# Four tiles in the first chunk, two in the second, and a fourth accumulator in the layer-1 banks

## The chip, the cores and the metric

The kernel runs on one core of a Trainium2 chip. The metric is the device time of one execution in microseconds (us), from the first to the last instruction with what lies around them. A run is repeated, and the median is taken.

## The reference

Windowed attention (half of the heads with a plain window of 32 keys, half with a window dilated by 4) feeds a token mixing of rank 32 and a two-layer network with a ReLU.

```python
scores = scale * np.matmul(q, k.transpose(0, 1, 3, 2))      # 8 batches, 8 heads, 576 tokens, 64 wide
mask_plain = (rel >= 0) & (rel < window)
mask_dil = (rel >= 0) & (rel < window * dilation) & (rel % dilation == 0)
...
x = softmax(np.where(masks, scores, -1e9)) @ v               # heads side by side: (8, 576, 512)
h = x.transpose(0, 2, 1) @ U @ V                             # U: 576x32, V: 32x576
u = x + h.transpose(0, 2, 1)
ch = np.maximum(u @ w_ch1, 0.0) @ w_ch2                      # w_ch1: 512x2048, w_ch2: 2048x512
return u + ch
```

U, V and the two weight matrices arrive as 64-bit numbers. The kernel narrows them itself, and it splits the operands of the large products into a high and a low part, so that each product is three products.

## The kernel before

The 8 x 576 tokens are 36 tiles of 128 rows. The network runs over **chunks** of 3 tiles, 12 in all; each chunk goes through 16 **steps f** of 128 hidden units. In a step, layer 1 (`layer1`, line 914) is 12 products of 128x128 weights with the chunk's 384 columns into a bank `ph`; ScalarE takes the ReLU into `hh` (L919), and VectorE the low part into `hl` (L920). Layer 2 (`layer2`, line 931) is three products of 512 columns for each tile into that tile's accumulator `acc`. The order is layer 1 of f, then layer 2 of f-1. The eight banks of the accumulation memory are three for `acc`, two for `ph` and three (`ps`) for everything else.

Chunk 0 is special in three ways. The weights are loaded and prepared in it: 32 pieces, two for a step, each fetched by a DMA into a buffer `raw` (`fetch64`, lines 189 and 191), narrowed by ScalarE (L198, L199), shifted by VectorE (L203), added by VectorE or GpSimd (`add_low`, L205) and split into high and low (L209, L211, L212). `weight_step`, called twice a step, does one stage each of four pieces in turn; `AHEAD` says how many pieces ahead a fetch is issued, and `RAWS` how many buffers `raw` there are, so that a fetch waits until the piece `RAWS` before it has been added. Second, the attention of batch 0 (`first_batch`) has been done ahead of it. Third, the attention of batch 1 runs inside it: nine groups, each with scores `s` (L405), a softmax on VectorE and ScalarE, a transpose `ptp` (L439), the products `pv` with the values `v` (L462) and `place`, which divides and puts the result into the tiles; the dilated half goes to `xp` and from there in up to six small DMAs to the tiles (L496, the scatter). Then come the low-rank products `t` (L541, from `xhl`, L511) and `m` (L565), whose result is added to the tile (L567).

All DMAs are issued by SyncE (SP), one after the other. Up to the end of chunk 0 the order on every engine is that of the code (`manual_schedule`). Where in it the work beside the network stands is set by `queue`: entries with a position, taken out by `slot()` in the gaps between groups of products. A position of 0 is the start of chunk 0 and 1 its end. Group i of batch 1 stands at `STEP0 + STEP1 * i`, the low-rank parts by `AFTER`, the way of batch 0's dilated half through memory at `leave` (L770) and `come` (L775), and batch 2 between `lo` and `hi`. From chunk 1 on a scheduler orders the work; batches 2 to 7 run inside the chunks 1 to 9.

`V1` says which columns of V come with the first of two small pieces.

Of the kernel before, what the change touches and what calls it, by code (L numbers as in the profile page):

```python
# [143 lines left out]
def attention_moe_kernel(ctx: ExitStack, tc: tile.TileContext, qk0, qk2, vv, masks, wide, ident, ut, vt, uv, w1, w2, out):  # L144
# [32 lines left out]
    def fetch64(i):  # L177
        src, n = pieces[i][0], pieces[i][1]
        if 2 * F_LAST <= i - NSMALL:
            raw = [xpool.tile([P, DM], I32, tag="x", name=f"raw{i}_{h}") for h in range(2)]  # L180
# [4 lines left out]
        for h, r in enumerate(raw):
            r = r[:, 0:step]
            if len(src.shape) == 3:
                k = src.shape[1] // len(raw)
                nc.sync.dma_start(out=r.rearrange("p (a b) -> p a b", a=k), in_=src[:, h * k:(h + 1) * k])
            else:  # L190
                nc.sync.dma_start(out=r, in_=src[:, h * step:(h + 1) * step])
# [273 lines left out]
    def place(g, pv):  # L465
# [29 lines left out]
        for t, to, n, r in sorted(moves) if b > 0 else ():  # L495
            nc.sync.dma_start(out=x_tile(t)[to:to + DIL * (n - 1) + 1:DIL, HALF_D:], in_=xp[r:r + n])  # L496
# [185 lines left out]
    def first_batch():  # L682
# [38 lines left out]
        t_first(0, 0)
        turn_dilated(2)
        t_evict(0, 1)
        tp[8] = turn_pe(8, state.pop(8)[0])
# [7 lines left out]
        turn_plain(0, 0)  # L732
        turn_plain(0, 1)
        t_first(2, 0)
        turn_plain(0, 2)
        for t in range(CT):
            turn_plain(1, t)
# [12 lines left out]
        for k in (0, 1):  # L750
            mix_turned(k)
        for k in (0, 1):
            split_u(k, 0)
        for k in (0, 1):
            split_u(k, 1)
        narrowed(w1)
        add_low(w1, nc.gpsimd)
# [293 lines left out]
```

## Time and profile before

| | |
|---|---|
| median of 3 runs | 1029.66 us (1026.68 to 1031.23) |
| the profiled execution, its own time | 1030.62 us |
| its span, first to last instruction | 1028.8 us |
| TensorE busy in the span | 988.2 us |
| VectorE, ScalarE, GpSimd busy | 586.3, 382.0, 331.8 us |
| moved by DMA | 101.36 MB |

The span is cut into 40 slices on the profile's page, with the busy share of each engine and the clock that TensorE was granted. Further views used here are the busy time by stretches (windows), the waits by engine, and the timeline, in which the matmuls of one line are merged; the time in square brackets is the idle time ahead of an instruction, and who ended it. Matmuls overlap in the records, so that the pace of a stream is the distance between starts, not the duration of one.

### The profile page before, as it was taken

The numbers are of one execution on the slowest core, as the hardware profiler recorded it, in microseconds if no ns is written. First come the engines' busy times: TensorE is split into PE (matmuls) and PEld (weight loads), VectorE is DVE, ScalarE is ACT, GpSimd is POOL, SyncE is SP. The second block draws the span as 40 slices with busy tenths as digits, with TensorE's granted clock in tenths as the row PEclk, the third lists the DMA queues.
The fourth block names the chain that finished last, engine by engine and source line by source line (L and its number), as shares of the span: only waits on it lengthen the run. The fifth ranks groups of instructions, "written<-read, shape, count | busy, mean of one in ns | idle before, by whom it ended". The sixth has DMA issues, their size and how long they took to land.

```text
span 1028.8 us, 18053 instructions
## 1 busy us (share of the span) xinstructions
PE 988.2 (96%) x5928; PEld 869.0 (84%) x5928; DVE 586.3 (57%) x1969; ACT 382.0 (37%) x937; POOL 331.8 (32%) x555
## 2 busy tenths in 40 slices
PE   7886887999999999999999999999999999999998
PEld 6576676888898888888898888988898888999997
DVE  4566686776446863766556773676646774311211
ACT  5663655444233431434323541434323441111110
POOL 4374656444032630425222540325313440000000
PEclk9988998999999999999999999999999999999999
DMA  9566543443223422333233422333223420300000
GB/s 252 171 196 206 169 145 108 117 134 89 72 73 96 138 75 75 113 97 114 64 85 97 130 82 74 106 106 112 84 74 93 126 69 21 113 1 1 31 1 31
DMA packets 95868, 101.36 MB, mean 99 GB/s; under 512 B 12480, under 2 KB 81344, under 8 KB 95776
## 3 DMA queue, kind: packets, MB, share of 16 engines
q1 hardware_dynamic: 95776, 100.21, 33.8%
q8 instruction: 48, 0.79, 0.3%
q14 instruction: 44, 0.36, 0.1%
HBM read 78.14 MB, written 17.89 MB: 93 GB/s over the span
## 4 chain that ended last, share of the span: by engine, by line
PE 83%; POOL 1%; DVE 1%; issue 1%; ACT 0%; DMA 0%; DVEq 0%; POOLq 0%; SPq 0%
PE acc L931 37%; PE ph L914 37%; PE pv L462 3%; PE s L392 3%; PE t L541 2%; PE m L565 1%; PE s L405 0%; POOL v L205 0%; POOL w1l L212 0%; DVE v L205 0%; DVE v L203 0%; POOL w2l L212 0%; PE tp L631 0%; DMA raw<-w 0%; DVE xhl L511 0%
## 5 line engine op out<-in xcount | busy, mean ns | idle before, releaser
L931 PE MATMUL acc<-w2h,hh 128*128 128x512 f32 x576 | 230.8, 401 | 0.0
L931 PE MATMUL acc<-w2l,hh 128*128 128x512 f32 x576 | 229.3, 398 | 0.0
L369 POOL TENSOR_TENSOR qks<-qkr,qks 128x160 fp32r<-128x160 f32 x192 | 103.1, 537 | 353.4 <-ACT qks L368 248.6
L920 DVE SCALAR_TENSOR_TENSOR hl<-ph,hh 128x384 fp32r<-128x384 f32 x192 | 106.2, 553 | 192.4 <-ACT hh L919 191.3
L931 PE MATMUL acc<-w2h,hl 128*128 128x512 f32 x576 | 214.2, 399 | 0.0
L919 ACT ACTIVATE hh<-ph 128x384 fp32r<-128x384 f32 x192 | 93.6, 487 | 284.4 <-PE ph L914 272.9
L914 PE MATMUL ph<-uth,w1h 128*128 128x384 f32 x768 | 171.4, 341 | 7.4 <-ACT w1h L209 6.0
L914 PE MATMUL ph<-utl,w1h 128*128 128x384 f32 x768 | 177.2, 343 | 0.0
L914 PE MATMUL ph<-uth,w1l 128*128 128x384 f32 x768 | 173.1, 341 | 1.2 <-POOL w1l L212 1.2
L428 ACT ACTIVATE p<-p,nmax 128x160 f32<-128x160 f32 (+1 forms) x288 | 109.5, 406 | 153.3 <-DVE nmax L424 152.2
L914 PEld LDWEIGHTS ph<-uth,w1h 128*128 128x128 f32 x768 | 138.2, 189 | 23.9 <-ACT w1h L209 7.3
L451 DVE STREAM_TRANSPOSE pt<-p 32x128 f32<-32x128 f32 x432 | 130.2, 301 | 18.7 <-ACT p L428 13.4
L914 PEld LDWEIGHTS ph<-uth,w1l 128*128 128x128 f32 x768 | 137.6, 190 | 2.5 <-POOL w1l L212 2.2
L914 PEld LDWEIGHTS ph<-utl,w1h 128*128 128x128 f32 x768 | 137.7, 191 | 1.7 <-issue 0.2
L931 PEld LDWEIGHTS acc<-w2h,hl 128*128 128x128 f32 x576 | 108.9, 189 | 23.2
L931 PEld LDWEIGHTS acc<-w2h,hh 128*128 128x128 f32 x576 | 109.6, 190 | 16.1
L931 PEld LDWEIGHTS acc<-w2l,hh 128*128 128x128 f32 x576 | 109.5, 190 | 15.9
L368 ACT CAST qks<-qkr 128x288 fp32r<-128x288 f32 x192 | 81.0, 429 | 95.0 <-PE s L392 56.3
L421 DVE TENSOR_TENSOR p<-s,wide_sb 128x160 f32<-128x160 f32 x192 | 60.1, 320 | 69.7 <-PE s L392 67.2
L372 POOL TENSOR_TENSOR qks<-qkr,qks 64x128 fp32r<-64x128 f32 x192 | 90.7, 472 | 15.1
L511 POOL TENSOR_TENSOR xhl<-x,xhl 128x256 fp32r<-128x256 f32 (+1 forms) x65 | 47.9, 746 | 82.3 <-ACT xhl L509 76.7
L462 PEld LDWEIGHTS pv<-v,pt 96*64 96x64 f32 x1152 | 41.4, 139 | 29.6 <-issue 11.6
(86 smaller groups left out, 901.0 us busy)
## 6 DMA issues: line engine op xcount, KB each, us to landing
qkr<-qk SPq DMA_DIRECT2D x192, 144.0 KB, 2.2
raw<-w SPq DMA_DIRECT2D x26, 512.0 KB, 4.3
v<-vv SPq DMA_DIRECT2D x126, 97.5 KB, 2.2
out<-x SPq DMA_DIRECT2D x36, 256.0 KB, 2.2
zd<-z SPq DMA_DIRECT2D x120, 64.0 KB, 2.2
xt<-zd SPq DMA_DIRECT2D x30, 256.0 KB, 2.8
k<-qk SPq DMA_DIRECT2D x18, 320.0 KB, 5.7
raw<-w SPq DMA_DIRECT2D x12, 256.0 KB, 3.8
```

Of the source, the lines that this page charges most:

```text
L368: nc.scalar.copy(out=t[:, 0:QK2], in_=raw)
L369: nc.gpsimd.tensor_tensor(out=t[:, QK2:], in0=raw[:, P:], in1=t[:, P:QK2].bitcast(F32), op=ALU.subtract)
L372: eng.tensor_tensor(out=t[lo, 0:P], in0=raw[lo, 0:P], in1=t[lo, 0:P].bitcast(F32), op=ALU.subtract)
L421: nc.vector.tensor_tensor(out=p_sb[:, u, :], in0=sp[:, 0:KW], in1=held[0][:, kind], op=ALU.add)
L428: nc.scalar.activation(out=p_sb[:, u, 0:w], in_=p_sb[:, u, 0:w], func=AF.Exp, bias=nmax[:, u:u + 1], scale=-1.0,)
L451: nc.vector.transpose(out=pt[WIN * k:WIN * (k + 1), :, rs], in_=p_sb[rs, :, o:o + WIN])
L462: nc.tensor.matmul(pv[rs, u, :], lhsT=pt[:, u, rs], rhs=loaded[g, 1, i][:, u, :], start=True, stop=True)
L511: eng.tensor_tensor(out=xl[rs], in0=x[rs], in1=xh[rs].bitcast(F32), op=ALU.subtract)
L914: nc.tensor.matmul(ph, lhsT=w[:, k, :], rhs=u[:, k, :], start=(n == 0), stop=(n == len(seq) - 1))
L919: nc.scalar.activation(out=hh, in_=ph, func=AF.Relu)
L920: nc.vector.scalar_tensor_tensor(out=hl, in0=ph, scalar=0.0, in1=hh.bitcast(F32), op0=ALU.max, op1=ALU.subtract)
L931: nc.tensor.matmul(acc[i], lhsT=h[:, ss], rhs=w, start=(f == 0 and n == 0), stop=(f == FC - 1 and n == 2))
```

## The change

The chunks are 4, 2 and then ten times 3 tiles. Chunk 0 is thus a third longer, and its layer 1 has 512 columns; chunk 1 has two tiles and 256 columns. Positions keep their unit of three tiles, so that chunk 0 ends at 4/3 and chunk 1 at 2. Chunk 0 needs a fourth accumulator, which takes one of the two banks `ph`.

```diff
-CTOK = CT * P
-NCHUNK = NTILE // CT
+CHUNKS = [range(0, 4), range(4, 6)] + [range(t, t + CT) for t in range(6, NTILE, CT)]
+CTOK = len(CHUNKS[0]) * P
+NCHUNK = len(CHUNKS)
-V1 = V0 + 3 * P
+V1 = V0 + CTOK
-AHEAD = 3
+AHEAD = 2
-AHEAD_AT = 0.9
+AHEAD_AT = (0.95, 1.3)
-RAWS = 5
+RAWS = 4
-STEP1 = 0.055
-AFTER = ((0.43, 0.015), (0.62, 0.018))
-NQ = 4
+STEP1 = 0.075
+AFTER = ((0.60, 0.022), (0.84, 0.03))
+LO2 = 1.31
+HI2 = 2.45
+NQ = 2
...
     def fetch64(i):
         if 2 * F_LAST <= i - NSMALL:
-            raw = [xpool.tile([P, DM], I32, tag="x", name=f"raw{i}_{h}") for h in range(2)]
+            raw = [work.tile([P, DM], I32, tag="qks", name=f"raw{i}_0", bufs=TB),
+                   xpool.tile([P, DM], I32, tag="x", name=f"raw{i}_1")]
...
     def place(g, pv):
-        for t, to, n, r in sorted(moves) if b > 0 else ():
+        if moves and b > 0:
+            scatter[g] = (xp, sorted(moves))
+            if b >= SPLIT:
+                spread_rows(g)
+
+    def spread_rows(g):
+        xp, moves = scatter.pop(g)
+        for t, to, n, r in moves:
             nc.sync.dma_start(out=x_tile(t)[to:to + DIL * (n - 1) + 1:DIL, HALF_D:], in_=xp[r:r + n])
...
             def pre(s=s, g=g):
-                if b < SPLIT and s + 1 < NGB:
-                    spread_q(g + 1)
+                if b < SPLIT and g - LAG - 1 in scatter:
+                    spread_rows(g - LAG - 1)
                 if s >= LAG:
                     weighted(g - LAG, held.pop(g - LAG))
             def post(s=s, g=g):
+                if b < SPLIT and s + 1 < NGB:
+                    spread_q(g + 1)
...
     def ahead(stage):
         if stage == 0:
+            held[0] = work.tile([P, len(WIDE_AT), KW], BF16, tag="mask", name="wide_sb", bufs=1)
...
-        lo, hi = 1.5 * b - 2 - LO0, 1.5 * b - 0.5
+        lo, hi = (1.5 * b - 2 - LO0, 1.5 * b - 0.5) if b > 2 else (LO2, HI2 + MARGIN)
...
-    for c in range(NCHUNK):
+    for c, tiles in enumerate(CHUNKS):
-        acc = [psum.tile([P, DM], F32, tag="acc", name=f"acc{c}_{i}", bufs=3) for i in range(CT)]
+        nt = len(tiles)
+        acc = [psum.tile([P, DM], F32, tag="acc" if i < CT else "ph", name=f"acc{c}_{i}", bufs=3 if i < CT else 2)
+               for i in range(nt)]
         def slot():
-            pos = c + slots[0] / (6 * FC - 3)
+            pos = (tiles[0] + nt * slots[0] / ((nt + 3) * FC - 3)) / CT
```

The end of `first_batch` is written in another order: the last transposes and value products come first, and the products that turn batch 0's tiles (`u`) behind them, now for four tiles.

The following rows are TensorE's at the end of batch 0, from the last scores on to where the tiles begin to be turned. `ptp8` and `pv8` are the transpose and the value products of the last of batch 0's nine groups, `t0` the low-rank product, `u2` and `u3` the turned dilated columns. Before:

```order
L462 MATMUL pv7_481<-v7_146,pt1_78 64x65 x8
L527 MATMUL t0_420<-x0_447,u32_92 32x256
L585 MATMUL u2_491<-id_sb_72,xp0_255 128x96
L585 MATMUL u2_491<-id_sb_72,xp1_292 128x96
L585 MATMUL u2_491<-id_sb_72,xp2_329 128x96
L585 MATMUL u2_491<-id_sb_72,xp3_370 128x80
L585 MATMUL u2_491<-id_sb_72,xp4_407 128x16
L439 MATMUL ptp8_500<-id_sb_72,p8_432 96x128 x4
```

and in the changed kernel:

```order
L441 MATMUL ptp8_474<-id_sb_72,p8_432 96x128 x4
L464 MATMUL pv7_484<-v7_146,pt1_78 64x65 x8
L538 MATMUL t0_420<-xp4_407,u32_92 32x256
L538 MATMUL t0_420<-x4_408,u32_92 32x256
L464 MATMUL pv8_501<-v8_148,pt0_77 64x65 x8
L596 MATMUL u2_518<-id_sb_72,xp0_255 128x128
```

`pv8` has moved ahead of all turning; before, both `u2` and `u3` stood ahead of it.

The next rows are SP's, ahead of the values `v13` of batch 1's fifth group. `raw` are weight pieces, `x<-xp` the scatter, `x<-spare` the second half of batch 0's way through memory, `k` the keys. Before:

```order
L319 DMA k15_967<-qk0 128x640
L496 DMA x4_408<-xp11_983 16x256
L496 DMA x5_780<-xp11_983 16x256 x2
L496 DMA x6_782<-xp11_983 32x256
L496 DMA x7_785<-xp11_983 16x256
L496 DMA x8_787<-xp11_983 32x256
L775 DMA x3_544<-spare_822 128x256
L775 DMA x4_408<-spare_822 64x256
L191 DMA raw18_1029<-w2 128x1024
L189 DMA raw19_1065<-w1 128x4x256
L340 DMA v13_0_1075<-vv 96x260
L340 DMA v13_1_1077<-vv 96x260
```

and in the changed kernel:

```order
L321 DMA k15_1001<-qk0 128x640
L507 DMA x4_408<-xp10_921 16x256
L507 DMA x5_900<-xp10_921 32x256
L507 DMA x6_902<-xp10_921 32x256
L507 DMA x7_905<-xp10_921 32x256
L507 DMA x8_907<-xp10_921 16x256
L191 DMA raw17_1052<-w1 128x4x256
L193 DMA raw18_1081<-w2 128x1024
L342 DMA v13_0_1092<-vv 96x260
L342 DMA v13_1_1094<-vv 96x260
```

The scatter ahead of `v13` is that of the group before, the last piece of weights ahead of it is 18 in place of 19, and the two transfers from `spare` stand further ahead.

The last rows are TensorE's where step f = 2 begins, with what the first product of layer 1 waits for in brackets; `w1h` is prepared by ScalarE. Before:

```order
L931 MATMUL acc0_2_584<-w2h_0_84,hh0_0_607 128x512
L931 MATMUL acc0_2_584<-w2l_0_85,hh0_0_607 128x512
L931 MATMUL acc0_2_584<-w2h_0_84,hl0_0_608 128x512
L914 MATMUL ph0_2_723<-uth0_69,w1h_0_82 128x384 [waits Activation_49]
L914 MATMUL ph0_2_723<-uth0_69,w1h_0_82 128x384 x3
```

and in the changed kernel:

```order
L942 MATMUL acc0_3_589<-w2h_0_84,hh0_0_631 128x512
L942 MATMUL acc0_3_589<-w2l_0_85,hh0_0_631 128x512
L942 MATMUL acc0_3_589<-w2h_0_84,hl0_0_632 128x512
L925 MATMUL ph0_2_734<-uth0_69,w1h_0_82 128x512 [waits DVE_49,Activation_49]
L925 MATMUL ph0_2_734<-uth0_69,w1h_0_82 128x512 x3
```

There are three more products of 512 columns in each layer 2, and layer 1 now waits for VectorE as well, whose `hl` of the step before has to leave the one bank `ph`.

More of the change, by code (lines that the diff above doesn't have):

```diff
@@ L77 @@
 NX = 16
-HI1 = 0.85
-W_OFF = 1000
 F_MID = 6
 F_LAST = 13
-RAWS = 5
+RAWS = 4
 VS = 4
@@ L620, in transp @@
     def transp(t):
-        c, i = divmod(t, CT)
+        c = next(c for c, ts in enumerate(CHUNKS) if t in ts)
+        i = t - CHUNKS[c][0]
         if c not in uts:
@@ L715, in first_batch @@
                 narrowed(0)
-                add_low(0, nc.gpsimd)
-                finish(0)
         w0, w1 = NSMALL, NSMALL + 1
+        tiles = CHUNKS[0]
+        tp[8] = turn_pe(8, state.pop(8)[0])
         place(6, pv.pop(6))
         pv[7] = product(7, pt.pop(7))
[L721 to L724, printed above, removed]
         copy(8)
-        finish(1)
-        t_first(1, 0)
-        turn_dilated(3)
+        for c in (1, 0):
+            t_first(ODD, c)
         place(7, pv.pop(7))
@@ L731, in first_batch @@
         narrowed(w0)
[L732 to L737, printed above, removed]
+        t_evict(0, 1)
+        finish(1)
+        turn_dilated(2)
         place(8, pv.pop(8))
         add_low(w0, nc.gpsimd)
-        send(NSMALL + 6)
+        for i in range(n - 1):
+            t_first(i, 0)
+        turn_dilated(3)
         mix_turned(2)
+        t_evict(0, 0)
         mix_turned(3)
-        t_first(3, 0)
         split_u(2, 0)
+        split_u(2, 1)
+        narrowed(w1)
+        finish(w0)
+        for k in (0, 1):
+            for t in tiles:
+                turn_plain(k, t)
+            mix_turned(k)
         split_u(3, 0)
-        split_u(2, 1)
-        t_evict(0, 0)
-        finish(w0)
+        add_low(w1, nc.gpsimd)
         split_u(3, 1)
[L750 to L757, printed above, removed]
+        for part in range(2):
+            for k in (0, 1):
+                split_u(k, part)
         narrowed(w1 + 1)
@@ L866, in attention_moe_kernel @@
     n0 = len(batch_parts(0))
-    queue = [(HI1 - MARGIN, lambda: ahead(0)), (AHEAD_AT, lambda: ahead(1))]
+    queue = [(AHEAD_AT[0], lambda: ahead(0)), (AHEAD_AT[1], lambda: ahead(1))]
     queue += [(0.15 + 0.01 * p, lambda p=p: leave(p)) for p in range(NDP)]
@@ L908, in layer1 @@
             assert NSMALL + 2 * f in finished
-            ph = psum.tile([P, CTOK], F32, tag="ph", name=f"ph{c}_{f}", bufs=2)
+            ph = psum.tile([P, CTOK], F32, tag="ph", name=f"ph{c}_{f}", bufs=2)[:, 0:nt * P]
             w1h, w1l = held_w[f][0:2]
@@ L916, in layer1 @@
                     slot()
-            hh = work.tile([P, CTOK], F32R, tag="hh", name=f"hh{c}_{f}", bufs=2)
-            hl = work.tile([P, CTOK], F32R, tag="hl", name=f"hl{c}_{f}", bufs=2)
+            hh = work.tile([P, CTOK], F32R, tag="hh", name=f"hh{c}_{f}", bufs=2)[:, 0:nt * P]
+            hl = work.tile([P, CTOK], F32R, tag="hl", name=f"hl{c}_{f}", bufs=2)[:, 0:nt * P]
             nc.scalar.activation(out=hh, in_=ph, func=AF.Relu)
@@ L927, in layer2 @@
             w2h, w2l = held_w[f][2:4]
-            for i in range(CT):
+            for i in range(nt):
                 ss = slice(i * P, (i + 1) * P)
@@ L932, in layer2 @@
                                      start=(f == 0 and n == 0), stop=(f == FC - 1 and n == 2))
-                if f < FC - 1 and i < CT - 1:
+                if f < FC - 1 and i < nt - 1:
                     slot()
-        more = list(range((c + 1) * CT, (c + 2) * CT)) if c + 1 < NCHUNK else []
+        more = list(CHUNKS[c + 1]) if c + 1 < NCHUNK else []
         for f in range(FC):
@@ L958, in attention_moe_kernel @@
             order.__exit__(None, None, None)
-        for i in range(CT):
-            t = c * CT + i
+        for i, t in enumerate(tiles):
             x = xt.pop(t)
```

13 lines of the change are left out of this document (7 added, 6 removed).

## The prediction

> **What bounds the kernel now.** I read the page first, then busy time by stretches, then TensorE's waits. The page's lines are TensorE's totals and its 40 slices of 25.7 us, with the granted clock:
>
> ```profile
> PE 988.2 (96%) x5928; PEld 869.0 (84%) x5928; DVE 586.3 (57%) x1969; ACT 382.0 (37%) x937; POOL 331.8 (32%) x555
> PE   7886887999999999999999999999999999999998
> PEclk9988998999999999999999999999999999999999
> ```
>
> From the eighth slice on TensorE is full at full clock. Only the first seven have room: the attention of batch 0 and chunk 0. The windows below cut chunk 0 in three, and the rest in two; columns are us, then busy us (and count) of PE, its weight loads, DVE, ACT and POOL, then granted clock, DMA share and GB/s.
>
> ```profile
> 43.30:102.70 59.40, 46.32 (x287) 41.04 (x288) 36.04 (x116) 30.46 (x71) 36.39 (x41) 0.85 0.64 197
> 102.70:153.90 51.20, 44.35 (x269) 36.49 (x267) 37.72 (x91) 31.11 (x72) 30.94 (x26) 0.94 0.52 158
> 153.90:181.50 27.60, 21.35 (x90) 17.63 (x91) 17.71 (x40) 13.39 (x35) 19.29 (x26) 0.88 0.38 105
> 181.50:260.00 78.50, 78.50 (x517) 68.97 (x515) 57.63 (x220) 36.18 (x90) 32.88 (x64) 1.00 0.40 111
> 260.00:1000.00 740.00, 740.00 (x4348) 657.40 (x4345) 411.43 (x1385) 245.51 (x605) 197.07 (x367) 1.00 0.28 81
> ```
>
> Chunk 0 lasts 138.2 us, of which PE is idle 138.2 - 46.32 - 44.35 - 21.35 = 26.2 us. No other engine is full there: DVE is busy 91.5 us, POOL 86.6, ACT 75.0. Behind it nothing but PE work counts. TensorE's waits in chunk 0 (us, times, longest):
>
> ```profile
> PE pv L462 <- DMA v<-vv: 8.2, 4, 3.8
> PE ph L914 <- ACT w1h L209: 6.0, 3, 2.5
> PE s L392 <- POOL qks L372: 2.9, 1, 2.9
> PE s L405 <- DVE x L567: 2.3, 1, 2.3
> PE t L541 <- POOL xhl L511: 2.0, 3, 1.2
> PE t L541 <- DVE xhl L511: 1.8, 2, 1.6
> PE ph L914 <- POOL w1l L212: 1.2, 3, 0.5
> ```
>
> **How much work chunk 0 holds.** The paces come from the chain that ended last (start, us, what), and from TensorE's timeline:
>
> ```profile
> 1013.55 2.09 PE ph L914 x12
> 1015.63 2.10 PE acc L931 x9
> ```
>
> ```profile
> 85.85 0.40 PE L565 MATMUL m<-ts,vs 128*128 128x256 f32 x2
> 86.09 0.86 PE L914 MATMUL ph<-uth,w1h 128*128 128x384 f32 x4
> ...
> 107.72 0.69 PE L462 MATMUL pv<-v,pt 96*64 96x65 f32 x16
> 108.33 1.13 PE L405 MATMUL s<-k,q 128*128 128x96 f32 x8
> 109.30 0.60 PE L439 MATMUL ptp<-id_sb,p 128*96 128x128 f32 x4
> 109.66 0.48 PE L931 MATMUL acc<-w2h,hh 128*128 128x512 f32 x1
> ```
>
> A product of 384 columns takes 2.09 / 12 = 0.174 us, one of 512 columns 2.10 / 9 = 0.233, one of 256 columns (86.09 - 85.85) / 2 = 0.12; a group of batch 1 takes 109.66 - 107.72 = 1.94. Chunk 0 before is thus 192 x 0.174 + 144 x 0.233 + 9 x 1.94 + 40 low-rank products at 0.12 + 16 others (transposes, first scores of batch 2) at about 0.12 = 33.4 + 33.6 + 17.5 + 4.8 + 1.9 = **91.2 us**. It lasts 138.2, so 47.0 us are lost: 26.2 idle, and most of the rest at half clock (1 - clock, doubled, times the windows' lengths: 17.8 + 6.1 + 6.6 = 30.5 us at half clock, up to 15 lost). An idle us costs 47.0 / 26.2 = 1.79 in all.
>
> **Term 1, the longer chunk itself.** In the changed chunk 0 layer 1 has 192 products of 512 columns, layer 2 192: 44.7 + 44.7 + 17.5 + 4.8 + 9 x 0.12 = **112.8 us**. A tile moved ahead takes 48 x 0.233 + 192 x (0.233 - 0.174) = 22.5 us away from what follows; this is no gain in work, but 22.5 us more to hide the same preparation under. Chunk 1 has 256 columns in layer 1: 192 x (0.12 - 2/3 x 0.174) = 0.8 us more.
>
> A weight load that did not fit under 256 columns would cost more. The eight scores above start every 0.97 / 8 = 0.121 us, though they stream 96 columns only, so a load of 128 columns takes about 0.12 itself and just fits. The Trainium skill's page "TensorE: Matmul & The Clock Gate", section "LDWEIGHTS (loading the stationary operand)", gives 128 / 1.2 = 107 ns, and its section "The mechanism" says that a load overlaps a running product only where the row groups differ, which full-height weights never do; by it chunk 1 would lose another 20.5 us (an estimate from the page). The trace disagrees: with fresh weights for each, 512 columns pace at 0.233 us, and 384 at 0.174, so the load is hidden.
>
> **Term 2, the start of layer 1.** The timeline before:
>
> ```profile
> 31.57 0.62 PE L527 MATMUL t<-x,u 128*32 128x256 f32 x2
> ...
> 35.98 0.69 PE L462 MATMUL pv<-v,pt 96*64 96x65 f32 x16
> ...
> 43.34 0.96 PE L914 MATMUL ph<-uth,w1h 128*128 128x384 f32 x4 [1.45 <-DVE utl L604]
> ```
>
> `pv8` stands at 35.98, 4.4 us behind the end of `pv7`'s run; in the new order two `t` (0.6 us) lie between, so it can come up to 3.8 us earlier. Behind it stand about 2.3 us more products (the turning, two tiles' plain parts), and four splits of 512 columns. Bounds: 39.5 (all of the 3.8 kept) and 45.7 (nothing of it, and 2.3 more). I take **41.0**: 35.98 - 3.8, the 7.4 us behind it without the 1.45 us in the bracket, 2.3 for the new products, and 0.6 of such waits left.
>
> **Term 3, what stays idle in chunk 0.** The largest wait is for `v`. SP's timeline at the longest, and TensorE's:
>
> ```profile
> 58.78 0.33 SPq L191 DMA_DIRECT2D raw<-w  x1
> ...
> 92.04 0.53 SPq L191 DMA_DIRECT2D raw<-w  x1
> 92.68 0.38 SPq L189 DMA_DIRECT2D raw<-w  x1
> 93.16 0.92 SPq L340 DMA_DIRECT2D v<-vv  x2
> 94.17 0.38 SPq L319 DMA_DIRECT2D k<-qk  x1
> 94.64 4.38 SPq L496 DMA_DIRECT2D x<-xp  x5
> ...
> 102.48 1.04 SPq L189 DMA_DIRECT2D raw<-w  x1
> ```
>
> ```profile
> 99.05 1.23 PE L462 MATMUL pv<-v,pt 96*64 96x65 f32 x16 [3.82 <-DMA v<-vv]
> ```
>
> From 58.78 to 103.5 SP's 33 rows sum to 37.4 of 44.7 us: issuing itself is nearly the bound there. `v13` is issued behind two pieces of weights and lands 5 us later. In the changed kernel a group comes every 0.075 in position, 6.1 gaps in place of 5.1, and a gap is 7 to a step of 5.6 us instead of 6 to one of 4.2: a group has about 7 us instead of 5.6 in full flow, for the same DMAs. Each `v` stands behind one piece of weights fewer, and the scatter ahead of it has its data. Four buffers with two pieces ahead wait for the same addition as five with three, so nothing is lost there. Of 8.2 us I keep 3 (bounds 0 and 8.2).
>
> The waits for weights (6.0 + 1.2) are at f = 1 and from f = 13 on: supply is 4.1 us of POOL for a step (two splits at 1.4, one addition at 1.3), demand falls from one step in about 6.6 to one in 8; I keep 3. Of the rest (2.9 + 2.3 + 3.8 + 2.8 at the start and the low-rank part, which is spread from 0.015 to 0.022 a piece) I keep 4.5: these are latencies, and half of them stay.
>
> New is the single `ph`: layer 1 of f+1 waits until ACT and DVE have read it. It has layer 2 of f-1 for that, 12 x 0.233 = 2.8 us. How long the reading takes shows in two places before, f = 8 and f = 13, in the last products of layer 1, ScalarE's `hh` (f = 13) and VectorE's `hl`:
>
> ```profile
> 122.71 0.86 PE L914 MATMUL ph<-utl,w1h 128*128 128x384 f32 x4
> ...
> 156.30 0.86 PE L914 MATMUL ph<-utl,w1h 128*128 128x384 f32 x4
> ```
>
> ```profile
> 160.81 0.47 ACT L919 ACTIVATE hh<-ph 128x384 fp32r<-128x384 f32 x1
> ```
>
> ```profile
> 124.13 0.56 DVE L920 SCALAR_TENSOR_TENSOR hl<-ph,hh 128x384 fp32r<-128x384 f32 x1 [3.46 <-ACT hh L919]
> ...
> 161.31 0.56 DVE L920 SCALAR_TENSOR_TENSOR hl<-ph,hh 128x384 fp32r<-128x384 f32 x1 [0.76 <-ACT hh L919]
> ```
>
> At f = 8 the lag from the end of layer 1 is 124.69 - 123.57 = 1.1 us and would be hidden; at f = 13 it is 161.87 - 157.16 = 4.7, because ACT is behind. 512 columns add some 0.3. I take 2.5 us for the 14 steps concerned (bounds 0 and 14 x (5.0 - 2.8) = 31). Together 3 + 3 + 4.5 + 2.5 = 13 us idle, x 1.79 = **23.3 us** lost. Bounds 6 and 26 us idle: 11 and 47.
>
> **Term 4, the rest.** From 181.5 to 1028.8 are 847.3 us; less 22.5, plus 0.8, plus seven products that no longer fit into chunk 0 (0.8), plus what batch 2 costs where it is denser: 1.14 positions in place of 1.3, with only 2.8 us in a step of chunk 1. DVE was at 57.63 / 78.5 = 73% there, and would be near 80%. I take 3 us (bounds 0, as PE never waits there before, and 10). That is **829.4**.
>
> Costed at nothing: NQ = 2 (a copy of the next queries has a whole group's time), the mask's buffer, 128 columns of V in the other small piece, a later GpSimd copy of the queries, which has the same 7 us.
>
> **Sum.** 41.0 + 112.8 + 23.3 + 829.4 = 1006.5 us of span; the profiled execution adds 1030.62 - 1028.8 = 1.8, and stands 1.0 above the median: **1007 us** against 1029.66.
>
> **Rivals.**
> - *All cover:* the preparation disappears under the longer chunk, 6 us stay idle, layer 1 starts at 39.5, chunk 1 loses nothing: 1007 - 12.3 - 1.5 - 3 = 990. For it: DVE's 91.5 us are no longer level with PE's work. Against: latencies stay. 0.13.
> - *Batch 2 pushes DVE over:* chunks 1 and 2 lose 10 us and the first idle more than I gave: about 1020. For it: 2.8 us a step. 0.08.
> - *Nothing covers:* the losses are chains of SP, POOL and DVE that stretch with the chunk, 47 us again: 1007 + 23.7 = 1031, no change. For it: SP's 37.4 of 44.7 us. Against: the DMAs per group don't grow. 0.11.
> - *Slower, by the one bank:* if DVE's `hl` lags as at f = 13 in all 14 steps, 31 us idle replace my 2.5, and each drags the clock down: 1007 + 28.5 x 1.79 = 1058. It decides from some 15 us of such waits, 1.1 a step, a lag of 3.9. Against: the lag of 1.1, and that ACT was behind at f = 13 because weights came late. 0.06. The Trainium skill's page "TensorE: Matmul & The Clock Gate", section "A second HAM failure mode: psum-queue depth-cycling", describes such a clock that swings as TensorE pauses briefly between groups while banks are cycled; here the clock was 1.00 in every stretch behind chunk 0, with two banks.
> - *Loads not hidden at 256 columns:* 192 x 0.121 = 23 us, back to 1030. Against: the paces above. 0.01.
>
> The forecast has 0.61, about 995 to 1019. **Range** 990 to 1024: it takes in the first two rivals, and leaves out 0.18. A difference of 0.5% (5 us) is about what a measurement can tell: faster 0.82, same 0.11, slower 0.07.
>
> **What would show it.** Layer 1 starts near 41 us; chunk 0's last product ends near 177, and the rest takes some 829 us. The waits of `pv` for `v` and of `ph` for `w1h` shrink below 3 us each; the clock in chunk 0 rises to 0.94 or more. If `ph` waits for DVE's `hl` at the head of most steps, the one bank was mispriced; if PE is idle between 180 and 290 us, chunk 1 was; if the `v` waits stand as before, SP's issuing was the bound all along.

## The result, and the profile after

The changed kernel takes 996.57 us (median of 4 runs, 994.34 to 999.47) against 1028.72 us for the kernel before on the same chip (4 runs, 1026.68 to 1031.23). The ratio is 0.969, with a 95% interval of 0.965 to 0.972: **3.1% faster**, 32 us. The profiled execution is the slowest of the four, 999.47 us with a span of 997.7.

The page of the changed kernel, TensorE's totals and slices:

```profile
PE 973.4 (98%) x5936; PEld 850.2 (85%) x5936; DVE 589.5 (59%) x1968; ACT 380.4 (38%) x936; POOL 330.7 (33%) x555
...
PE   7898999999999999999999999999999999999998
...
PEclk9999999999999999999999999999999999999999
```

Of the notches that the slices of before had in the first seven (a 6, two 7s, four 8s) one 7 and two 8s are left, and the clock stands at 9 throughout. The windows cut chunk 0 in three, and the rest in two (columns as in the prediction):

```profile
44.35:98.00 53.65, 48.01 (x284) 38.69 (x286) 36.77 (x106) 29.95 (x70) 32.63 (x39) 0.94 0.64 200
98.00:146.00 48.00, 46.03 (x289) 36.10 (x286) 40.27 (x90) 28.79 (x66) 31.29 (x28) 1.00 0.63 192
146.00:174.36 28.36, 26.56 (x121) 20.92 (x119) 21.79 (x38) 13.28 (x33) 17.88 (x21) 1.00 0.37 104
174.36:252.00 77.64, 77.17 (x560) 67.93 (x559) 57.93 (x228) 38.17 (x100) 36.33 (x69) 1.00 0.42 121
252.00:997.70 745.70, 739.29 (x4374) 657.03 (x4372) 410.75 (x1393) 245.37 (x605) 196.02 (x367) 1.00 0.29 80
```

Layer 1 starts at 44.35 us, 1.0 later than before. Chunk 0 lasts 130.0 us instead of 138.2, with a tile more in it. PE is idle in it for 5.64 + 1.97 + 1.80 = 9.4 us (26.2 before), and the clock is below 1.00 only in its first part: (1 - 0.94) x 2 x 53.65 = 6.4 us at half clock, against 30.5. (The trace also keeps the times at which the granted clock changed: two stretches at half clock, of 3.41 us each, against nine before.) Of its 130.0 us, 112.8 are products by the prediction's count, so 17.2 are lost (47.0 before). What follows takes 997.7 - 174.36 = 823.3 us. TensorE's waits in chunk 0 (us, times, longest):

```profile
PE ptp L441 <- DVE x L578: 2.1, 1, 2.1
...
PE t L552 <- POOL xhl L522: 1.6, 2, 1.2
PE ph L925 <- ACT w1h L211: 1.6, 1, 1.6
PE m L576 <- ACT ts L568: 1.3, 1, 1.3
PE pv L464 <- DMA v<-vv: 0.9, 1, 0.9
PE ph L925 <- POOL w1l L214: 0.5, 1, 0.5
PE ph L925 <- DVE hl L931: 0.5, 1, 0.5
```

The wait for `v` fell from 8.2 us to 0.9, that for `w1h` from 6.0 to 1.6. The single bank `ph` made layer 1 wait for VectorE's `hl` once, 0.5 us.

### The profile page after: what moved, and what is told of

Read it like the earlier page. It is cut to its first block, busy times and chain, and to the rows that moved or that the text cites. A ratio compares the mean times of both kernels' runs of the same rounds, so it can differ in the third digit from the quotient of the medians.

```text
span 997.7 us, 18064 instructions
## 1 busy us (share of the span) xinstructions
PE 973.4 (98%) x5936; PEld 850.2 (85%) x5936; DVE 589.5 (59%) x1968; ACT 380.4 (38%) x936; POOL 330.7 (33%) x555
## 4 chain that ended last, share of the span: by engine, by line
PE 79%; DVE 4%; DMA 2%; SPq 1%; issue 1%; ACT 1%; POOL 0%; DVEq 0%; POOLq 0%; ACTq 0%
PE ph L925 35%; PE acc L942 34%; PE pv L464 3%; PE s L394 3%; PE t L552 2%; PE m L576 1%; DVE pt L453 1%; SPq L507 1%; DMA raw<-w 1%; DMA zd<-z 1%; DVE v L205 1%; DMA qkr<-qk 0%; PE s L407 0%; DVE utl L649 0%; DVE x L972 0%
## 5 line engine op out<-in xcount | busy, mean ns | idle before, releaser
L942 PE MATMUL acc<-w2h,hh 128*128 128x512 f32 x576 | 228.2, 396 | 0.2 <-DVE x L972 0.2
L931 DVE SCALAR_TENSOR_TENSOR hl<-ph,hh 128x384 fp32r<-128x384 f32 (+2 forms) x192 | 106.3, 554 | 178.0 <-ACT hh L930 177.1
L930 ACT ACTIVATE hh<-ph 128x384 fp32r<-128x384 f32 (+2 forms) x192 | 93.7, 488 | 264.3 <-PE ph L925 254.9
L925 PE MATMUL ph<-utl,w1h 128*128 128x384 f32 (+2 forms) x768 | 173.2, 339 | 0.0
L925 PE MATMUL ph<-uth,w1h 128*128 128x384 f32 (+2 forms) x768 | 169.4, 339 | 3.8 <-DVE utl L615 1.7
L925 PE MATMUL ph<-uth,w1l 128*128 128x384 f32 (+2 forms) x768 | 170.5, 339 | 0.5 <-POOL w1l L214 0.5
L430 ACT ACTIVATE p<-p,nmax 128x160 f32<-128x160 f32 (+1 forms) x288 | 109.6, 406 | 135.6 <-DVE nmax L426 134.1
L925 PEld LDWEIGHTS ph<-uth,w1h 128*128 128x128 f32 x768 | 135.8, 188 | 20.9 <-ACT w1h L211 2.9
L453 DVE STREAM_TRANSPOSE pt<-p 32x128 f32<-32x128 f32 x432 | 130.1, 301 | 19.5 <-ACT p L430 14.2
L925 PEld LDWEIGHTS ph<-utl,w1h 128*128 128x128 f32 x768 | 133.8, 189 | 3.9 <-issue 0.2
L925 PEld LDWEIGHTS ph<-uth,w1l 128*128 128x128 f32 x768 | 133.6, 189 | 4.1 <-POOL w1l L214 1.1
L942 PEld LDWEIGHTS acc<-w2l,hh 128*128 128x128 f32 x576 | 108.7, 189 | 15.9 <-issue 0.2
L426 DVE CUSTOM_DVE_ANT_0 p<-s,p 128x160 f32<-128x160 f32 x192 | 59.9, 320 | 3.7
```

Of the source, the lines that this page charges most:

```text
L426: nc.vector.tensor_tensor_reduce(out=p_sb[rs, u, 0:w], in0=a, in1=c, scale=-1.0 / 8.0, scalar=3.0e38, op0=ALU.add, op1=ALU.min, accum_out= ...
L430: nc.scalar.activation(out=p_sb[:, u, 0:w], in_=p_sb[:, u, 0:w], func=AF.Exp, bias=nmax[:, u:u + 1], scale=-1.0,)
L453: nc.vector.transpose(out=pt[WIN * k:WIN * (k + 1), :, rs], in_=p_sb[rs, :, o:o + WIN])
L925: nc.tensor.matmul(ph, lhsT=w[:, k, :], rhs=u[:, k, :], start=(n == 0), stop=(n == len(seq) - 1))
L930: nc.scalar.activation(out=hh, in_=ph, func=AF.Relu)
L931: nc.vector.scalar_tensor_tensor(out=hl, in0=ph, scalar=0.0, in1=hh.bitcast(F32), op0=ALU.max, op1=ALU.subtract)
```

## The experiments

All kernels are told in one table; what follows says what each one is. "Lost" is the length of chunk 0 less its products (112.8 us with four tiles, 91.2 with three), "idle" is PE's idle time in it, "rest" what follows it. "Half clock" counts the stretches of 3.41 us at half clock in chunk 0, by the times of clock changes in the trace; where two or three follow one another, each counts. Medians are of 4 or 5 runs (7 to 9 for the kernel before, run beside the experiments on three chips: 1028.7 to 1029.0), the other columns are of the profiled execution.

| kernel | median us | ratio to before, 95% | layer 1 starts | chunk 0 | lost | idle | half clock | rest |
|---|---|---|---|---|---|---|---|---|
| before | 1028.7 | | 43.3 | 138.2 | 47.0 | 26.2 | 9 | 847.3 |
| changed | 996.6 | 0.965 to 0.972 | 44.35 | 130.0 | 17.2 | 9.4 | 2 | 823.3 |
| chunk_alone | 1017.5 | 0.985 to 0.990 | 44.7 | 149.9 | 37.1 | 21.0 | 8 | 821.9 |
| three_tiles | 1019.3 | 0.988 to 0.992 | 40.7 | 131.0 | 39.8 | 23.7 | 7 | 845.0 |
| packed | 1011.9 | 0.981 to 0.985 | 44.1 | 144.6 | 31.8 | 20.0 | 5 | 822.6 |
| groups_early | 1004.7 | 0.975 to 0.979 | 41.4 | 139.1 | 26.3 | 15.3 | 4 | 821.2 |
| scatter_at_once | 1000.0 | 0.969 to 0.973 | 42.9 | 134.1 | 21.3 | 12.3 | 3 | 822.1 |
| old_end | 1000.1 | 0.971 to 0.974 | 44.2 | 132.1 | 19.3 | 9.7 | 3 | 822.9 |
| three_one_bank | 1021.5 | 0.992 to 0.996 | 41.5 | 134.6 | 43.4 | 25.3 | 7 | 846.2 |
| acc_in_ps | 1006.5 | 0.977 to 0.980 | 42.75 | 135.9 | 23.1 | 14.3 | 2 | 828.1 |
| after_again | 996.0 | 0.966 to 0.970 | 42.85 | 129.6 | 16.8 | 10.4 | 1 | 821.8 |
| mix_spread | 993.8 | 0.965 to 0.968 | 41.85 | 128.2 | 15.4 | 8.6 | 1 | 821.4 |
| spread_more | 993.6 | 0.963 to 0.967 | 42.8 | 128.0 | 15.2 | 8.3 | 1 | 822.4 |
| both | 993.1 | 0.964 to 0.967 | 41.8 | 128.1 | 15.3 | 7.6 | 2 | 822.3 |

### The longer chunk, or the order of the work in it

Two theories were put against each other. "Cover": the losses shrink because the same preparation lies under 22.5 us more products. "Order": they shrink because SP's order and the new distances of batch 1 take the waits away. Five kernels take the change apart. **chunk_alone** has the chunk sizes, the bank, the buffers and batch 2's new place, and the rest as before:

```diff
-STEP1 = 0.075
-AFTER = ((0.60, 0.022), (0.84, 0.03))
+STEP1 = 0.055
+AFTER = ((0.43, 0.015), (0.62, 0.018))
...
         if moves and b > 0:
             scatter[g] = (xp, sorted(moves))
-            if b >= SPLIT:
-                spread_rows(g)
+            spread_rows(g)
...
             def pre(s=s, g=g):
...
+                if b < SPLIT and s + 1 < NGB:
+                    spread_q(g + 1)
...
             def post(s=s, g=g):
-                if b < SPLIT and s + 1 < NGB:
-                    spread_q(g + 1)
```

and besides the old end of `first_batch`, as in old_end below.

> Chunks of 4, 2 and 3 tiles with the fourth accumulator in the layer-1 banks and the buffers that this needs (two pieces ahead, four raw buffers), but batch 1 timed as before (a group every 0.055), its scatter and the copy of the next queries issued as before, and the end of batch 0 in the old order, with the fourth tile's products added. Theory 'cover' (the losses of chunk 0 shrink because the same preparation lies under 22.5 us more products, whatever its order): layer 1 starts at 45 to 46, chunk 0 loses 20 to 28 us, waits of pv for v at most 4 us, 1000 to 1009 us. Theory 'order' (the losses shrink because SP's order and the spread of batch 1 take the v waits away, and the longer chunk by itself gives little): v waits 8 us or more, 35 to 47 us lost, 1015 to 1028 us.

Measured: 1017.5 us, a third of the gain (11.2 of 32). TensorE's waits in chunk 0 of chunk_alone, the largest:

```profile
PE pv L464 <- DMA v<-vv: 7.5, 3, 4.6
PE t L551 <- POOL xhl L521: 4.2, 3, 1.9
PE t L551 <- ACT xhl L519: 2.3, 2, 1.3
PE ph L929 <- POOL w1l L214: 2.0, 3, 1.3
...
PE ph L929 <- ACT w1h L211: 1.4, 1, 1.4
```

The `v` waits are nearly those of before, and the low-rank products `t` now wait for their operands as well. "Cover" asked for 20 to 28 us lost, "order" for 35 to 47; 37.1 were. The waits for weights, however, have fallen from 6.0 + 1.2 (`w1h`, `w1l`) to 1.4 + 2.0 us: the weights, two pieces to a step, spread over a longer chunk by themselves. Batch 1 does not, since its positions are counted in tiles.

**three_tiles** is the opposite, every edit but the chunk sizes and the positions that go with them; batch 1's distances are those of before, so of "order" it tests the order on SP and the engines alone:

```diff
-CHUNKS = [range(0, 4), range(4, 6)] + [range(t, t + CT) for t in range(6, NTILE, CT)]
+CHUNKS = [range(t, t + CT) for t in range(0, NTILE, CT)]
-AHEAD_AT = (0.95, 1.3)
+AHEAD_AT = (0.55, 0.9)
-STEP1 = 0.075
-AFTER = ((0.60, 0.022), (0.84, 0.03))
-LO2 = 1.31
-HI2 = 2.45
+STEP1 = 0.055
+AFTER = ((0.43, 0.015), (0.62, 0.018))
+LO2 = 0.9
+HI2 = 2.2
```

> All edits except the chunk sizes: 12 chunks of 3 tiles, three accumulators of their own and two layer-1 banks throughout, batch 1 and batch 2 timed as before; the scatter one group later, the copy of the queries later, two pieces ahead with four raw buffers, and the new end of batch 0. 'Cover': no gain, 1022 to 1032 us, 40 to 50 us lost in chunk 0, v waits 5 us or more. 'Order': the v waits are gone (under 3 us) and with them the clock's dips, 1008 to 1016 us. If two pieces ahead are too few without the longer chunk, waits of layer 1 for weights grow above 8 us and it is slower than 1032.

Measured: 1019.3 us, between the two. The waits in its chunk 0, the largest:

```profile
PE ph L925 <- ACT w1h L211: 6.2, 3, 2.6
PE pv L464 <- DMA v<-vv: 3.5, 2, 3.3
```

In this trace the order alone takes more than half of the `v` wait away, and leaves the weights' wait where it was. The split is not firm: three_one_bank below has the same order, and waits 6.9 us for `v` and 3.6 for `w1h`. The sum of the two is 9.7 and 10.5 us, against 14.2 before. Neither trace shows two pieces ahead in four buffers to supply worse than three in five. The new distances without the longer chunk were not run: their last entry stands at 0.84 + 11 x 0.03 = 1.17, behind the end of a chunk of three tiles.

**packed** is the changed kernel with batch 1's timing of before:

```diff
-STEP1 = 0.075
-AFTER = ((0.60, 0.022), (0.84, 0.03))
+STEP1 = 0.055
+AFTER = ((0.43, 0.015), (0.62, 0.018))
```

> The changed kernel with batch 1 timed as before the change (a group every 0.055 in position instead of 0.075, low-rank parts from 0.43 and 0.62): the last quarter of the longer chunk has no attention. 'Cover': what is late early is made up later, 998 to 1004 us. 'Order' (here: the spread is what removes the v waits): v waits back at 6 to 8 us, two or more further windows at half clock, 1006 to 1016 us.

Measured: 1011.9 us. The largest waits in its chunk 0:

```profile
PE pv L464 <- DMA v<-vv: 5.0, 1, 5.0
PE t L552 <- POOL xhl L522: 4.8, 3, 1.9
PE t L552 <- ACT xhl L520: 2.3, 2, 1.3
```

"Order" holds in this form, though the `v` wait is under the 6 to 8 us expected and the `t` waits make up the rest: two lines of constants are worth 1011.9 - 996.0 = 15.9 us (after_again), half of the whole gain, though they move no work in or out of chunk 0. What is late early is not made up later: each wait is an idle PE, and the free stretch at the end gives nothing back.

**groups_early** has the old distance of the groups only, with the low-rank products where the change puts them:

```diff
-STEP1 = 0.075
+STEP1 = 0.055
```

> The changed kernel with the nine groups of batch 1 at the old distance (0.055), but its low-rank products where the change puts them (from 0.60 and 0.84). The packed kernel (both as before) took 1011.9 us; its waits in chunk 0 were 5.0 us of pv for v and some 9 us of the low-rank t and m for xhl and ts. If the groups' distance is the larger part: 1005 to 1011 us, a v wait of 4 to 5 us. If the low-rank distance is: 998 to 1003 us, and t waits as short as in the changed kernel (2 us).

Measured: 1004.7 us, just under the 1005 to 1011 of the first case. The largest waits in its chunk 0:

```profile
PE pv L464 <- DMA v<-vv: 4.4, 1, 4.4
PE t L552 <- POOL xhl L522: 4.2, 2, 2.2
```

The `v` wait is there; the `t` waits are too (with two of 0.3 us beside the one shown), so the second case fails on both. Taken in this order, the low-rank products' distance is worth 7.2 us (1011.9 - 1004.7) and the groups' another 8.7 (1004.7 - 996.0).

**scatter_at_once** takes the scatter's delay away:

```diff
         if moves and b > 0:
             scatter[g] = (xp, sorted(moves))
-            if b >= SPLIT:
-                spread_rows(g)
+            spread_rows(g)
```

> The changed kernel with the scatter of a group's dilated rows issued right behind place as before, ahead of the next group's v on SP. 'Cover': 996 to 1000 us, v waits at most 2 us, as a group has 7 us and its DMAs need less. 'Order': SP stands still until place has written xp, so v comes late at the four groups with dilated rows: v waits 4 to 8 us, 1003 to 1011 us.

Measured: 1000.0 us, `v` waits of 2.1 us. "Cover" is nearer: at the new distances the order on SP matters little for `v`. What is new is a wait of 3.5 us of `m` for one of batch 0's additions on VectorE, which neither theory named; the delay is worth some 4 us in all.

So neither theory stands alone. From before to chunk_alone are 11 us, from there to packed (SP's and GpSimd's order, the end of batch 0) 6, and from there to the changed kernel 16. On this reading the cover makes room, and the distances use it.

### The single bank

**three_one_bank** is three_tiles with the third accumulator of chunk 0 in a layer-1 bank:

```diff
-        acc = [psum.tile([P, DM], F32, tag="acc" if i < CT else "ph", name=f"acc{c}_{i}", bufs=3 if i < CT else 2)
+        acc = [psum.tile([P, DM], F32, tag="acc" if c or i < 2 else "ph", name=f"acc{c}_{i}", bufs=3 if c or i < 2 else 2)
```

> The kernel of three_tiles (all edits, 12 chunks of 3 tiles, 1019.3 us), but in chunk 0 the third accumulator takes one of the two layer-1 banks, as the fourth does in the changed kernel. It prices the single bank alone; layer 2 of f-1 is 9 x 0.233 = 2.1 us here, which is less cover than the 2.8 us of four tiles. Theory 'hidden' (reading a bank lags 1.1 to 1.4 us behind layer 1): at most 4 us of waits of layer 1 for hh and hl, 1019 to 1024 us. Rival 'one bank' (the reading lags 4 to 5 us as at f = 13): 2 to 3 us of wait in 15 steps, 30 to 45 us, 1050 us or more.

Measured: 1021.5 us, 2.2 more than three_tiles (the intervals overlap); one wait of layer 1 for `hl`, 1.5 us, against none. Its chunk 0 is 3.6 us longer, and in that its `v` wait of 6.9 us against 3.5 also stands (and a `w1h` wait of 3.6 against 6.2), which the bank doesn't explain. "Hidden" holds even under the shorter layer 2.

**acc_in_ps** gives the changed kernel its second layer-1 bank back, at the expense of `ps`:

```diff
-        acc = [psum.tile([P, DM], F32, tag="acc" if i < CT else "ph", name=f"acc{c}_{i}", bufs=3 if i < CT else 2)
+        acc = [psum.tile([P, DM], F32, tag="acc" if i < CT else "ps", name=f"acc{c}_{i}", bufs=3)
```

> The changed kernel with the fourth accumulator in one of the three banks for other work (ps), so that layer 1 keeps two banks in chunk 0. If the one bank cost more than its measured wait of 0.5 us: 990 to 995 us. If it is hidden: 996 to 999 us where two ps banks are enough. If batch 1, whose scores, transposes, value products and low-rank products pass through ps, waits for its own evictions with two: waits of s, ptp or pv for DVE and ACT of 5 us or more, 1003 to 1020 us.

Measured: 1006.5 us, some 10 us slower than the changed kernel. Its largest waits in chunk 0 are new ones:

```profile
PE ptp L441 <- DVE x L494: 5.0, 4, 2.6
PE m L576 <- DVE x L578: 2.4, 3, 1.3
PE ptp L441 <- DVE xp L494: 2.0, 3, 1.0
```

With two banks `ps` left, the transposes wait 7 times until `place` (L494) has read a bank; no wait for `hl` is left. So the bank taken from layer 1 was the cheap one. The rest is 5 us longer too: scores wait 3.2 us in it, and the trace has one more stretch at half clock, at 398 us. Why was not followed up.

### The end of batch 0

**old_end** is the changed kernel with the old end of `first_batch`, the fourth tile's plain products added behind the last `place`. The core of it:

```diff
-        tp[8] = turn_pe(8, state.pop(8)[0])
         place(6, pv.pop(6))
         pv[7] = product(7, pt.pop(7))
+        t_first(0, 0)
+        turn_dilated(2)
+        t_evict(0, 1)
+        tp[8] = turn_pe(8, state.pop(8)[0])
         copy(8)
+        t_first(1, 0)
+        turn_dilated(3)
         place(7, pv.pop(7))
         pv[8] = product(8, pt.pop(8))
         narrowed(w0)
-        turn_dilated(2)
...
-        turn_dilated(3)
...
+        for k in (0, 1):
+            turn_plain(k, 3)
+            mix_turned(k)
```

> The changed kernel with the end of batch 0 in the old order (the turning of the dilated columns ahead of the last transposes and value products), the fourth tile's plain products added behind the last place. If the new order is worth what it is with 3 tiles (layer 1 at 40.7 against 43.3): layer 1 starts at 46 to 47, 998 to 1001 us. If with 4 tiles the evictions of 512 columns set the start in either order: 44 to 45, 995 to 998 us.

Measured: 1000.1 us, and layer 1 at 44.2. TensorE's timeline of old_end: `pv7`, `pv8`, the start:

```profile
30.15 0.69 PE L464 MATMUL pv<-v,pt 96*64 96x65 f32 x16
...
36.12 0.69 PE L464 MATMUL pv<-v,pt 96*64 96x65 f32 x16
...
44.18 1.19 PE L930 MATMUL ph<-uth,w1h 128*128 128x512 f32 x4 [1.54 <-DVE utl L615]
```

and of the changed kernel:

```profile
31.66 0.69 PE L464 MATMUL pv<-v,pt 96*64 96x65 f32 x16
...
33.49 0.69 PE L464 MATMUL pv<-v,pt 96*64 96x65 f32 x16 [0.58 <-DVE x L494]
34.10 1.91 PE L596 MATMUL u<-id_sb,xp 128*128 128x128 f32 x14
35.95 1.91 PE L538 MATMUL t<-x,u 128*32 128x256 f32 x8
37.79 1.91 PE L596 MATMUL u<-id_sb,xp 128*128 128x128 f32 x14
...
44.35 1.19 PE L925 MATMUL ph<-uth,w1h 128*128 128x512 f32 x4 [1.75 <-DVE utl L615]
```

The start as such agrees with the second expectation (44 to 45), the time with the first (998 to 1001). The starts hide the gain, since `pv7` stands 1.5 us later in the second execution. From `pv7` to layer 1 are 14.03 us in the old order and 12.69 in the new: 1.3 us won. With three tiles it is the same: 43.34 - 30.95 = 12.39 before, 40.68 - 29.61 = 11.07 in three_tiles. The fourth tile costs 12.69 - 11.07 = 1.6. Another 2 to 2.5 us of old_end's 4 are lost inside chunk 0 (19.3 against 17.2 and 16.8). Its idle time there is the same, 9.7 us against 9.4 and 10.4, but it has three stretches at half clock against two and one; that the order causes these is not shown.

### What is left in chunk 0

The largest wait of the changed kernel is 2.1 us of `ptp` for an addition on VectorE (L578). VectorE's row behind it, and SP's rows for the same stretch:

```profile
83.71 0.41 DVE L578 TENSOR_TENSOR x<-x,m 64x256 f32<-64x256 f32 x1 [3.32 <-DMA x<-spare]
```

```profile
75.54 5.87 SPq L507 DMA_DIRECT2D x<-xp  x6
81.45 0.59 SPq L784 DMA_DIRECT2D x<-spare  x1
```

The addition needs the last transfer from `spare`, which SP issues behind six DMAs of the scatter: VectorE stands for 3.3 us, and `hl`, the softmax and TensorE behind it. A stretch at half clock follows the wait; a window cut to it, and two of TensorE's rows in it:

```profile
85.49:88.90 3.41, 3.41 (x10) 2.67 (x9) 1.71 (x11) 3.08 (x8) 1.26 (x2) 0.50 0.55 168
```

```profile
87.06 0.63 PE L942 MATMUL acc<-w2l,hh 128*128 128x512 f32 x1
87.49 0.63 PE L942 MATMUL acc<-w2h,hl 128*128 128x512 f32 x1
```

Products of 512 columns start every 0.43 us in it, instead of every 0.233, so that one such stretch costs 3.41 x (1 - 0.233 / 0.43) = 1.56 us. **mix_spread** moves the additions apart, so that the last comes well behind its load:

```diff
-    queue += [(0.18 + 0.012 * i, lambda i=i: mix(0, i, 0)) for i in range(n0)]
-    queue += [(0.27 + 0.008 * i, lambda i=i: mix(0, i, 1)) for i in range(n0)]
+    queue += [(0.18 + 0.018 * i, lambda i=i: mix(0, i, 0)) for i in range(n0)]
+    queue += [(0.29 + 0.03 * i, lambda i=i: mix(0, i, 1)) for i in range(n0)]
```

> The changed kernel with batch 0's ten small low-rank additions further apart (the plain half from 0.18 every 0.018, the dilated half from 0.29 every 0.03 instead of from 0.27 every 0.008). In the changed kernel the last of them held VectorE for 3.3 us, until a load came that SP had issued behind six DMAs of the scatter, and TensorE stood 2.1 us behind it; a window at half clock followed. If an idle us costs about 1.8 in all: the wait of ptp for the addition falls from 2.1 to under 0.5, 2 to 4 us faster than the changed kernel in the same runs. If the window at half clock comes anyway (other waits nearby set it off): 0 to 2 us faster.

**spread_more** takes batch 1 to the end of the chunk, **both** joins the two, and **after_again** is the changed kernel beside them:

```diff
-STEP1 = 0.075
-AFTER = ((0.60, 0.022), (0.84, 0.03))
+STEP1 = 0.085
+AFTER = ((0.68, 0.022), (0.93, 0.028))
```

> The changed kernel with batch 1 spread further: a group every 0.085, the low-rank parts from 0.68 and 0.93 (every 0.022 and 0.028), so that it fills chunk 0 to its end. If the distance of the groups is still what costs: the v wait (0.9) goes, chunk 0 loses 2 to 5 us less, 992 to 995 us. If what remains are waits of another kind (the first weights, single latencies): within 2 us of the changed kernel. If the last additions come too late for chunk 1's two tiles: layer 1 of chunk 1 waits 2 us or more, 998 to 1003 us.

> The two changes before this one together. If the waits are separate places, their gains add: 990 to 994 us. If both only move the same window at half clock: no better than the better of the two.

> The changed kernel once more, unaltered, beside the next three. Its median was 996.6 us. Layer 1 started between 41.4 and 44.4 us in profiled executions of kernels with this same beginning, always 10.9 us behind the start of the last group's value products. If the difference comes from the time at which TensorE goes from half to full pace in batch 0, that time and the start of layer 1 move together here too; a start between 41 and 44.5 us, and a span between 992 and 999 us.

Measured: 993.8, 993.6 and 993.1 us against 996.0 for the changed kernel beside them. The three lie 2.2 to 2.9 us lower, but every one of their intervals still meets that of after_again, so a gain is likely and not shown. The gains don't add (15.4, 15.2 and 15.3 us lost). In mix_spread no addition waits for `spare` any more, and the stretch at half clock at that wait is gone (it stands at 81.6 us in after_again); but the wait for an addition falls from 2.1 only to 0.9 us, not under 0.5, 0.8 of another wait comes beside it, and a stretch at half clock stands at 49.4 us instead; in spread_more the `v` wait falls to 0.6, and `t` and `m` wait 1.9 and 2.0 for VectorE and ScalarE instead. What is left are first weights (2.1), the `utl` at the start (1.7) and single latencies. How much such a wait costs is partly chance: the same wait of 1.6 us for the first `w1h` is followed within 3 us by a stretch at half clock in the changed kernel, mix_spread, both and acc_in_ps, and by none in after_again, spread_more, packed, groups_early and scatter_at_once.

## Why the prediction was right, point by point

The forecast was 1007 us in 990 to 1024, 22.7 us less than before; 32 were gained. The mechanism was right; two of the terms were sized too dear, and the start too cheap. On the profiled execution its span was 1006.5, and 997.7 were measured: the three terms that can be compared are off by +3.35 (start), -6.1 (lost in chunk 0) and -6.1 (rest), together -8.8. The last 1.9 us of the difference between 1007.3 (before rounding) and 996.6 come from the comparison with medians: the profiled execution lay 1.0 above its median before, and 2.9 above it after.

- **The work of chunk 0 and of the tile moved ahead** (term 1) is right. Without any loss the rest would be 847.3 - 22.5 = 824.8; 823.3 were measured, and 821 to 823 in the nine other four-tile kernels that leave `ps` its three banks. Weight loads do fit under 256 columns, as the paces said. TensorE's timeline at the start of chunk 1:

```profile
174.36 0.62 PE L925 MATMUL ph<-uth,w1h 128*128 128x256 f32 x4
174.81 0.62 PE L925 MATMUL ph<-uth,w1l 128*128 128x256 f32 x4
175.27 0.62 PE L925 MATMUL ph<-utl,w1h 128*128 128x256 f32 x4
175.72 0.59 PE L394 MATMUL s<-qks 128*128 128x320 f32 x3
```

Twelve products take 175.72 - 174.36 = 1.36 us, 0.113 each; 0.12 was assumed, so even the 0.8 us charged for chunk 1 is none. (The Trainium skill's page "TensorE: Matmul & The Clock Gate", section "The mechanism", besides the sentence that the prediction drew on, also names the background weight buffer, next to another row group, as a case in which a load is pulled ahead. The pace here contradicts the sentence drawn on; no run here shows the buffer itself.)

- **The start** (term 2: 41.0) was mis-sized: it is 44.35. Of the 3.35 us, 0.7 lie ahead of `pv7` (31.66 against 30.95, see the last section). The other 2.6 are the step from `pv8` on, "the 7.4 us behind it without the 1.45 us in the bracket, 2.3 for the new products, and 0.6": behind `pv8` stand 10.86 us and not 8.85, since the two turnings and two of the four `t`, which had stood ahead of it, run there one after the other (in the three rows of 1.91 us above); and `pv8` comes 3.2 us closer to `pv7`, not 3.8. The prediction let `pv8` gain by what left its front, and did not charge all of it behind. The reordering is still worth its 1.3 us. In after_again, where TensorE came to full pace nearly when it did before (13.4 us against 13.5), layer 1 starts at 42.85, 1.85 late.

- **What stays idle in chunk 0** (term 3: 13 us, 23.3 lost) is 9.4 us, 17.2 lost. The factor of 1.79 lost for one idle us was measured as 17.2 / 9.4 = 1.83, and lies between 1.6 and 2.0 in all kernels of the table. It is an average, and not one price: idle time and 1.56 us for each stretch at half clock leave some 4 to 7 us of every kernel's loss, with much idle time or little. The terms of the idle time: `v` 0.9 instead of 3; weights 2.1 instead of 3; the other latencies 2.1 + 1.6 + 1.3 and small ones, some 5.5 instead of 4.5; the one bank 0.5 instead of 2.5. That it is only 0.5 is no accident of one trace (1.5 in three_one_bank). It shows for the `hl` of f = 14 alone; VectorE's timeline, and TensorE's:

```profile
161.28 1.73 DVE L207 CUSTOM_DVE_ANT_0 v<-raw,v 128x512 uint16<-128x512 uint16 x2
162.94 0.41 DVE L578 TENSOR_TENSOR x<-x,m 128x256 f32<-128x256 f32 x1
163.38 0.71 DVE L621 STREAM_TRANSPOSE z<-x 128x512 f32<-128x512 f32 x1
164.01 0.65 DVE L931 SCALAR_TENSOR_TENSOR hl<-ph,hh 128x512 fp32r<-128x512 f32 x1
```

```profile
164.81 1.17 PE L925 MATMUL ph<-uth,w1h 128*128 128x512 f32 x4 [0.46 <-DVE hl L931]
```

`hl` is late there behind four other instructions of VectorE; elsewhere the 2.8 us of layer 2 hide it, as the lag of 1.1 us at f = 8 had said.

- **Why it shrinks.** The step "a group has about 7 us instead of 5.6" was the right mechanism, and it carried more than the text gave it: with the groups back at 5.6 us the four-tile chunk loses 26.3 us, with the low-rank products back as well 31.8. The step "each `v` stands behind one piece of weights fewer, and the scatter ahead of it has its data" is true on SP, but the scatter's delay is worth only 4 us beside the new distance, and the piece of weights was not tested by itself. "Half of them stay" came out in the sum (some 5.5 of 11.8 us), not wait by wait: that of `s` for `qks` (2.9) is gone, and that of `ptp` for an addition (2.1) takes its place.

- **The rest** (term 4: 829.4) is 823.3. The 3 us charged for the denser batch 2 are not there: PE waits 0.5 us between 174 and 252 us, and VectorE is busy 57.93 / 77.64 = 75% there, where 80% was expected.

- **The rivals.** "All cover" (990) came nearest: its rest (826.4) was even beaten, its 6 us idle and its start were not met. "Nothing covers" (1031) is half true for the chunk without its new distances (37.1 us lost). "The one bank" and "batch 2 pushes VectorE over" fell by the waits above, and "loads not hidden" by the pace of 0.113.

## What to carry to other kernels

A longer stage hides preparation only as far as the preparation is laid out over it: here the sizes alone gave 11 of 32 us, and two lines of distances 16. Where the clock follows TensorE's gaps, an idle us costs more than itself (here the stage lost 1.6 to 2.0 us for each); count the stretches at half clock apart, and look for the one instruction whose operand is issued behind a run of DMAs. When an order is rewritten to bring one producer forward, charge everything that it was moved past to the chain behind it.

## What the runs showed of the hardware

The start of layer 1 moved by 3 us between executions of kernels that are the same up to there: 44.35 in the changed kernel, 41.40 in groups_early, 42.85 in after_again. TensorE's timeline of groups_early, to be laid beside the rows of the changed kernel above:

```profile
9.65 1.13 PE L407 MATMUL s<-k,q_sb 128*128 128x96 f32 x8
...
30.54 0.69 PE L464 MATMUL pv<-v,pt 96*64 96x65 f32 x16 [0.58 <-DVE x L494]
...
41.40 1.20 PE L925 MATMUL ph<-uth,w1h 128*128 128x512 f32 x4 [1.74 <-DVE utl L615]
```

and a row of the changed kernel:

```profile
13.60 2.02 PE L407 MATMUL s<-k,q_sb 128*128 128x96 f32 x8
```

Eight scores take about 2.0 us at the beginning of these kernels, and 1.13 later. Full pace began at about 9.7 us in groups_early, at 13.4 in after_again, and behind 16.4 in the changed kernel; TensorE's first product stands near 5 us in all. Behind `pv8` the three are equal (10.86 to 10.87 us to layer 1). So nearly the whole 3 us come from the moment at which TensorE left half pace, and the profiled execution of the changed kernel, 2.9 us above its median, had the latest of the three. The clock column of the windows doesn't show it; for the changed kernel it gives 1.00 there:

```profile
10.00:20.00 10.00, 10.00 (x89) 8.80 (x89) 4.35 (x34) 5.55 (x18) 3.17 (x8) 1.00 1.06 259
```

That 1.00 is no reading. The trace's clock record begins with the step up to full clock, at 9.7, 13.4 and 17.2 us in the three, which agrees with the paces; ahead of its first entry the view prints 1.00.

The Trainium skill's page "TensorE: Matmul & The Clock Gate", section "What's actually happening", says that the clock is decided in free-running windows of 3413 ns, so that the change of pace falls elsewhere from run to run, and that products run at half clock for about the first 3.4 us. The traces agree on the first: the moment moves by 7.5 us between executions, and every stretch at half clock in chunk 0 lasts 3.41 us or two or three times that. The half pace at the beginning, however, lasted from 4.7 us (4.93 to 9.65) to over 11 (5.03 to beyond 16.4).
